# Storing the weight gradients of a decode block from GpSimd's queue instead of ScalarE's

## The chip, the cores and the metric

The kernel runs on one core of a Trainium2 chip. A core has five engines that each work through their own instructions in order: TensorE (PE in the profile, with its weight loads as PEld), VectorE (DVE), ScalarE (ACT), GpSimd (POOL) and SyncE (SP). They wait for each other by semaphores. Data move between the chip's memory (HBM) and the core's on-chip memory (SBUF) by DMA: an engine's sequencer issues a transfer into a DMA queue, sixteen DMA engines carry it out, and a semaphore tells when it has landed. SP's transfers go into queue q1 of the profile, ACT's into q10, and POOL's into q0.

The metric is the time of one execution on the device in microseconds (us), the median of several. Lower is better.

## The reference

One decode step of a small transformer block, forward and backward, in bfloat16. There are two sequences (B = 2) of one token each, a model width D of 640, 32 heads of 128, a cache of 4096 positions and an MLP of width 1728. Cut to what matters:

```python
def _A_ref(x, k_cache, v_cache, wq, wo):        # attention against a cache
    q = (x @ wq)  ->  heads
    p = softmax(q . k * 128**-0.5)
    return (p . v) @ wo
def _B_ref(x, w1, w2):                          # MLP
    return relu(x @ w1) @ w2

h   = x + _A_ref(layernorm(x), k_cache, v_cache, wq, wo)
out = h + _B_ref(layernorm(h), w1, w2)
# returned: out, and the gradients of (x, k_cache, v_cache, wq, wo, w1, w2) for a given grad_out
```

The caches have the shape 2 x 32 x 4096 x 128, so K, V and their two gradients are 64 tiles of 1 MB each, and these 256 MB are most of the traffic. The gradients of the four weights are outer products of rows that belong to the two tokens: `wq` (640 x 4096), `wo` (4096 x 640), `w1` (640 x 1728) and `w2` (1728 x 640). Together they are 15 MB, and it is their stores that the change touches.

## The kernel before

The work goes through the 64 pairs of sequence and head. In the first part (alone up to about 255 us, then beside the second) each pair's K and V are loaded (`Kt`, `Vt`), the scores are made by transposing K on TensorE (L440, copied out of PSUM by ACT in L445) and multiplying (L453), and the head's output is summed (L476). In the second part (`p2_iter`) V is loaded a second time for each pair (`Wt`), except for twelve pairs whose tile was kept. From it come the gradients of the probabilities (again L440, L445, L453 into `dp_ps`), from these the scores' gradient `gsp` on DVE (L874), and then the two 1 MB tiles `gK` and `gV`, which DVE writes (L860) and `store` (L881) sends out. From about 455 us on only the second part runs.

Beside this main line run three generators, of which a few steps are taken after each step of the main line (`bg_step`), by credits that are counted when the program is written. The order of the instructions on each engine is therefore fixed. One of the generators, `fin_gen`, makes the weight gradients once the values they need are there. It turns columns into rows (`rows_of`, L973, L978, L980), and `outer_rows` or `w2_rows` takes a tile `ot` of up to 1 MB, fills it piece by piece by `outer_tile` (TensorE multiplies into `o_ps`, L998, and ACT casts that into `ot`, L1004), and stores the tile when it is full (L1007). There are 19 such stores. Another generator, `gx_gen`, loads `wq` again in five tiles `wqs` (L1084) and multiplies them on DVE (`gxj`, L694), eight instructions to a tile.

What sets the order around the change:

- **Queues.** From about 490 us on (`alone`), `load_queue` is GpSimd's, so that `Wt`, `wqs` and `w_t` (L461, L1084, L380, L383) are issued by POOL, and the stores of `gK` and `gV` go through SP. Before that it is the other way round. The stores of `ot` are issued by ACT. POOL otherwise copies small vectors (`pp`, L905, and `pa`, L909) for the main line.
- **Buffers.** Tiles of 1 MB come from a stock that is shared out by purpose: `ld` for loads, `g` for `gK` and `gV`, `f` for `ot` (one at first, three later), `q` for `wqs`, `w_t` and two rows. An instruction that takes a tile waits until its last user, a store for instance, is done with it.
- **Completion semaphores.** In the built program every transfer signals one of eight semaphores, in turn, and a new transfer first waits until the last one with the same semaphore has landed. The transfers of SP and ACT share one set of eight; POOL's have a set of eight to themselves.

Of the kernel before, what the change touches and what calls it, by code (L numbers as in the profile page):

```python
# [15 lines left out]
def kernel(  # L16
# [20 lines left out]
    nc = tc.nc  # L37
# [35 lines left out]
    def pst(shape, dtype, role, name):  # L73

        k = banks[role].pop(0)
        banks[role].append(k)
        return ps.tile(shape, dtype, tag=f"bank{k}", bufs=1, name=name)
# [29 lines left out]
    def give(t, to=None, out=False):  # L107
        tag, k, _ = home_of.pop(id(t))
        if out:
            stored.add(k)  # L110
        to = to or goes_to(tag)
        owned[tag] -= 1
        owned[to] += 1
        free[to] += 1
        homes[to].append(k)
        given_at[k] = step[0]
# [872 lines left out]
    def outer_tile(todo, L, R, ot, stores):  # L989

        made = []
        for x in range(len(todo) + 1):
            if x < len(todo):
                sl, P, k, n0, nn = todo[x]
                q = 32 * (fw[0] % 4)
                o_ps = pst([128, 512], FP32, "o", "o_ps")
                fw[0] += 1
                nc.tensor.matmul(o_ps[0:P, 0:nn], lhsT=L[q:q + B, sl], rhs=R[q:q + B, n0:n0 + nn],  # L998
                                 start=True, stop=True)
                made.append((o_ps, P, k, n0, nn))  # L1000
                yield 0.3
            if x > 0:
                o_ps, P, k, n0, nn = made[x - 1]
                nc.scalar.copy(out=ot[0:P, k, n0:n0 + nn], in_=o_ps[0:P, 0:nn])  # L1004
                yield 0.3
        for out_ap, src in stores:
            nc.scalar.dma_start(out=out_ap, in_=src)  # L1007
        give(ot, out=True)

    def outer_rows(L, nrow, R, N, out_ap, cc):  # L1010


        P = nrow // cc
        grp = max(1, min(cc, 4096 // N))
        out_v = out_ap.rearrange("(p c) n -> p c n", c=cc)
        for c0 in range(0, cc, grp):
            gn = min(grp, cc - c0)
            while not rested("f", 13):
                yield 0.0
            ot = take("f", [128, grp, N], "ot")  # L1020
            todo = [(bass.ds(c0 + k, P, step=cc), P, k, n0, min(512, N - n0))
                    for k in range(gn) for n0 in range(0, N, 512)]
            yield from outer_tile(todo, L, R, ot, [(out_v[:, c0:c0 + gn, :], ot[0:P, 0:gn, :])])

    def w2_rows(L, R):

        out_v = out_7[0:NFF * 128, :].rearrange("(p c) n -> p c n", c=NFF)
        c0 = 0
        for gn in (5, 4, 4):
            while not rested("f", 13):  # L1030
                yield 0.0
            ot = take("f", [128, 6, D], "ot")
            last = c0 + gn == NFF
            cs = [(bass.ds(c0 + k, 128, step=NFF), 128, k) for k in range(gn)]
            if last and F_rem:
                cs.append((slice(NFF * 128, Dff), F_rem, gn))
            todo = [(sl, P, k, n0, min(512, D - n0)) for sl, P, k in cs for n0 in range(0, D, 512)]
            stores = [(out_v[:, c0:c0 + gn, :], ot[:, 0:gn, :])]
            if last and F_rem:
                stores.append((out_7[NFF * 128:Dff, :], ot[0:F_rem, gn, :]))  # L1040
            yield from outer_tile(todo, L, R, ot, stores)
            c0 += gn
# [314 lines left out]
```

## Time and profile before

| | |
|---|---|
| time of the kernel before | 888.31 us, median of 3 runs (886.6 to 888.36) |
| the profiled execution | 889.79 us, of which the span from the first to the last instruction is 888.0 us |
| busy: PE, DVE, ACT, POOL | 83%, 77%, 56%, 20% of the span |
| moved by DMA | 361.86 MB, 407 GB/s over the span |
| by queue: q1 (SP), q0 (POOL), q10 (ACT) | 264.49, 80.86 and 14.92 MB |
| granted TensorE clock | 0.773 on average, 0.5 to 0.7 from 490 us on |

An instruction in the profile has the line of the kernel, the engine, the operation and the tiles as out<-in. "Idle before <-releaser" is the time for which the engine had nothing to do, with what ended it. The DMA row gives the share of the sixteen DMA engines that were at work, in tenths for each of forty equal slices of 22.2 us, and as a fraction (1.00 is all sixteen) where a stretch of time is asked for; it can come out a little over 1, since packets of one engine can overlap. Beside the issue of a transfer the trace also has its sixteen signals of completion, one from each DMA engine.

### The profile page before, as it was taken

The numbers are of one execution on the slowest core, as the hardware profiler recorded it, in microseconds if no ns is written. First come the engines' busy times: TensorE is split into PE (matmuls) and PEld (weight loads), VectorE is DVE, ScalarE is ACT, GpSimd is POOL, SyncE is SP. The second block draws the span as 40 slices with busy tenths as digits, with TensorE's granted clock in tenths as the row PEclk, the third lists the DMA queues.
The fourth block names the chain that finished last, engine by engine and source line by source line (L and its number), as shares of the span: only waits on it lengthen the run. The fifth ranks groups of instructions, "written<-read, shape, count | busy, mean of one in ns | idle before, by whom it ended". The sixth has DMA issues, their size and how long they took to land.

```text
span 888.0 us, 24782 instructions
## 1 busy us (share of the span) xinstructions
PE 737.1 (83%) x10143; PEld 616.3 (69%) x10143; DVE 681.1 (77%) x1281; ACT 497.5 (56%) x1292; POOL 176.6 (20%) x309
## 2 busy tenths in 40 slices
PE   4999899899999998969858867878877898757593
PEld 4888788788887887858748756666666666544462
DVE  2666788877888886976778887878787779979763
ACT  1344343346777664645436868777656766545463
POOL 1344433443311000000022211110100211211000
PEclk9999999999999998999985556555556756556555
DMA  9999999999989999999999999999999999999986
GB/s 378 425 418 414 417 409 417 424 424 411 354 301 414 424 425 424 422 426 425 406 400 394 415 423 411 419 420 416 422 412 394 424 427 422 426 426 427 424 358 279
DMA packets 56146, 361.86 MB, mean 407 GB/s; under 512 B 5680, under 2 KB 11568, under 8 KB 15328
## 3 DMA queue, kind: packets, MB, share of 16 engines
q1 hardware_dynamic: 41640, 264.49, 72.0%
q0 software_dynamic: 11168, 80.86, 22.1%
q10 hardware_dynamic: 3224, 14.92, 4.1%
q8 instruction: 80, 1.31, 0.5%
q14 instruction: 34, 0.28, 0.1%
HBM read 211.11 MB, written 149.13 MB: 406 GB/s over the span
## 4 chain that ended last, share of the span: by engine, by line
DMA 37%; PE 35%; DVE 15%; ACT 7%; issue 4%; SPq 0%; ACTq 0%; POOL 0%; DVEq 0%; POOLq 0%
DMA Vt<-in_A_v_cache_dram 15%; PE t_ps L440 15%; DMA out_dram<-gK 11%; PE m_ps L476 8%; DMA out_dram<-gV 7%; DVE gK L860 4%; ACT gV L950 3%; DVE gV L860 3%; PE s_ps L453 3%; DMA wqs<-in_A_wq_dram 2%; DVE pk L486 2%; PE u_ps L514 2%; ACT t_sb L445 2%; PE dp_ps L453 2%; DVE gxj L694 1%
## 5 line engine op out<-in xcount | busy, mean ns | idle before, releaser
L445 ACT COPY t_sb<-t_ps 128x512 f32<-128x512 f32 x479 | 272.9, 587 | 194.3 <-PE t_ps L440 185.5
L453 PEld LDWEIGHTS <-t_sb 128*128 128x128 bf16 x4096 | 178.4, 102 | 66.5 <-ACT t_sb L445 39.6
L440 PE MATMUL t_ps<-ident_f,Wt 128*128 128x128 f32 x832 | 198.9, 390 | 1.1 <-ACT t_sb L445 1.1
L486 DVE TENSOR_TENSOR pk<-Kt,ep 128x2048 bf16<-128x2048 bf16 (+1 forms) x128 | 152.6, 1192 | 46.1 <-ACT ep L540 29.5
L476 PE MATMUL m_ps<-pk,Vt 128*128 128x129 bf16 x2048 | 171.0, 222 | 20.2 <-DMA Vt<-in_A_v_cache_dram 19.1
L860 DVE TENSOR_TENSOR gK<-rb,gsp 128x2048 bf16<-128x2048 bf16 x128 | 152.7, 1221 | 16.0 <-DMA out_dram<-gV 10.8
L476 PEld LDWEIGHTS <-Vt 128*128 128x128 bf16 x2048 | 124.7, 99 | 50.6 <-issue 28.6
L440 PEld LDWEIGHTS t_ps<-ident_f,Wt 128*128 128x128 f32 x832 | 138.6, 202 | 28.9 <-issue 22.0
L440 PE MATMUL t_ps<-ident_f,Kt 128*128 128x128 f32 x1024 | 155.0, 285 | 4.0 <-DMA Kt<-in_A_k_cache_dram 3.6
L860 DVE TENSOR_TENSOR gV<-rb,pp 128x2048 bf16<-128x2048 bf16 (+1 forms) x128 | 143.1, 1142 | 16.1 <-DMA out_dram<-gK 11.5
L453 PE MATMUL dp_ps<-gom,t_sb 128*128 128x2 bf16 x2048 | 95.9, 168 | 28.0 <-ACT t_sb L445 27.6
L440 PEld LDWEIGHTS t_ps<-ident_f,Kt 128*128 128x128 f32 x1024 | 113.2, 144 | 6.7 <-PE s_ps L453 3.9
L502 POOL COPY pk<-ep 128x16 bf16<-128x16 bf16 x80 | 84.5, 1058 | 155.7 <-ACT ep L540 80.9
L453 PE MATMUL s_ps<-qm,t_sb 128*128 128x2 bf16 x2048 | 87.4, 164 | 1.2 <-DVE t_sb L443 1.2
L1004 ACT CAST ot<-o_ps 128x512 bf16<-128x512 f32 (+3 forms) x152 | 67.7, 491 | 8.1 <-PE o_ps L998 5.3
L604 ACT CAST MT<-m_ps 128x128 bf16<-128x128 f32 x64 | 17.0, 265 | 93.4 <-PE m_ps L476 93.3
L461 POOL DMA_DIRECT2D Wt<-in_A_v_cache_dram x37 | 19.9, 539 | 223.3 <-PE t_ps L440 129.9
L903 ACT ACTIVATE rb<-dp_ps,rt 128x256 bf16<-128x256 f32 x64 | 30.2, 472 | 40.8 <-PE dp_ps L898 40.1
L694 DVE CUSTOM_DVE_ANT_0 hbc<-wo_t,hbc 128x640 bf16<-128x640 bf16 x64 | 52.7, 824 | 0.3
L874 DVE SCALAR_TENSOR_TENSOR gsp<-dp_ps,negdot,P_bf 128x64 bf16<-128x64 f32 x64 | 17.8, 278 | 45.0 <-PE dp_ps L453 45.0
L694 DVE CUSTOM_DVE_ANT_0 gxj<-wqs,gqr 128x1024 bf16<-128x1024 bf16 x40 | 48.8, 1220 | 1.6 <-DMA wqs<-in_A_wq_dram 1.5
L950 ACT ACTIVATE gV<-rb,pa 128x128 bf16<-128x128 bf16 x152 | 46.5, 392 | 4.6 <-DMA out_dram<-gK 4.1
(208 smaller groups left out, 752.8 us busy)
## 6 DMA issues: line engine op xcount, KB each, us to landing
Kt<-in_A_k_cache_dram SPq DMA_DIRECT2D x64, 1024.0 KB, 18.0
Vt<-in_A_v_cache_dram SPq DMA_DIRECT2D x64, 1024.0 KB, 17.3
out_dram<-gK SPq DMA_DIRECT2D x48, 1024.0 KB, 16.0
out_dram<-gV SPq DMA_DIRECT2D x47, 1024.0 KB, 17.0
Wt<-in_A_v_cache_dram POOLq DMA_DIRECT2D x37, 1024.0 KB, 11.2
out_dram<-gV POOLq DMA_DIRECT2D x17, 1024.0 KB, 9.8
out_dram<-gK POOLq DMA_DIRECT2D x16, 1024.0 KB, 10.4
Wt<-in_A_v_cache_dram SPq DMA_DIRECT2D x15, 1024.0 KB, 14.2
```

What stands on the lines that cost most here:

```text
L440: nc.tensor.transpose(t_ps[:, j, :], natf[:, 2 * cc:2 * cc + 2, :].rearrange("p c k -> p (c k)"), ident_f[:])
L445: nc.scalar.copy(out=t_sb[:], in_=t_ps[:])
L453: nc.tensor.matmul(dst[:, sc:sc + 2], lhsT=v[:, j, :, par], rhs=vecs[:, par, :], start=(par == 0), stop=(par == 1))
L461: load_queue().dma_start(out=t[:], in_=natural(A_k_cache if what == "K" else A_v_cache, *(turns if what == "W" else pairs)[i]))
L476: nc.tensor.matmul(r["m"][:, 0:129], lhsT=r["V"][:, sc, :], rhs=r["pk"][sc // HALF][:, sc % HALF, 0:129], start=(sc == 0), stop=(sc == NSC ...
L486: nc.vector.tensor_tensor(out=p["pk"][k][:, 0:n, 0:128].rearrange("p s (a two) -> p s a two", two=2), in0=p["K"][:, sl, :].rearrange("p s ...
L502: nc.gpsimd.tensor_copy(out=col, in_=e)
L694: nc.vector.tensor_tensor_reduce(out=junk[0:kc, 0:width], in0=in0, in1=in1, scale=1.0, scalar=0.0, op0=ALU.mult, op1=ALU.add, accum_out=acc)
L860: nc.vector.tensor_tensor(out=pairs_view(dst[:, sl, :]), in0=row.rearrange("p (a two) -> p a two", two=2)[:, None, :, :].to_broadcast([128 ...
L903: nc.scalar.activation(out=rb[:], in_=bank[:, 128:384], func=ACT.Copy, scale=rt[:, b, h:h + 1])
L950: nc.scalar.activation(out=gV[:, NSC - act + k, :], in_=c["rb"][:, 0:128], func=ACT.Copy, scale=pa[:, k:k + 1])
L1004: nc.scalar.copy(out=ot[0:P, k, n0:n0 + nn], in_=o_ps[0:P, 0:nn])
```

## The change

One line is changed. The store of a finished `ot` tile is issued by GpSimd's queue and not by ScalarE's.

```diff
@@ outer_tile @@
         for out_ap, src in stores:
-            nc.scalar.dma_start(out=out_ap, in_=src)
+            nc.gpsimd.dma_start(out=out_ap, in_=src)
         give(ot, out=True)
```

In the built program the 19 stores leave ACT's instructions and stand among POOL's, between the loads and copies that were issued around them; nothing else moves on any engine. A store now waits on POOL for ACT's last cast and for a semaphore of POOL's set; it shares queue q0 with the loads; and the eight semaphores that ACT and SP shared are SP's alone, but for the two small loads at the start.

## The prediction

> **What bounds the kernel now.** I read the page's DMA row first. All sixteen DMA engines are nearly always at work, so what matters is where they are not.
>
> ```profile
> DMA  9999999999989999999999999999999999999986
> GB/s 378 425 418 414 417 409 417 424 424 411 354 301 414 424 425 424 422 426 425 406 400 394 415 423 411 419 420 416 422 412 394 424 427 422 426 426 427 424 358 279
> ```
>
> The stores in question run from 567 us to the end, slices 26 to 40. There the ceiling of about 426 GB/s is held but for two slices near 660 us and the last two. So next come stretches of the end (columns: window, its length, then each engine's busy time, granted clock, DMA share, GB/s).
>
> ```profile
> 800.00:840.00 40.00, 25.99 (x204) 16.79 (x202) 35.09 (x54) 19.78 (x39) 4.00 (x7) 0.57 1.01 425
> 840.00:858.00 18.00, 14.96 (x132) 11.26 (x133) 10.04 (x11) 10.75 (x24) 0.47 (x2) 0.50 0.95 397
> 859.30:861.30 2.00, 2.00 (x16) 1.06 (x14) 0.79 (x2) 1.49 (x4) 0.00 (x0) 0.50 0.10 41
> 862.00:868.00 6.00, 5.57 (x43) 3.81 (x41) 3.42 (x4) 4.55 (x10) 0.00 (x0) 0.50 1.02 418
> 869.20:870.80 1.60, 1.60 (x9) 0.83 (x9) 1.60 (x2) 1.32 (x4) 0.00 (x0) 0.50 0.06 26
> 884.00:886.30 2.30, 0.00 (x0) 0.00 (x0) 0.00 (x0) 0.00 (x0) 0.00 (x0) 0.50 0.06 25
> ```
>
> The reader is to see the shares of 0.10 and 0.06. One engine of sixteen is 0.0625, and 425/16 is 26.6 GB/s: where fifteen DMA engines run dry, one goes on at full rate, to the very end. The sixteen completion signals of each store say the same. For the `gK` store issued at 863.18, fifteen came by 867.1 and the last at 873.1; for the one at 667.30, by 673.0 and at 682.1; for the one at 749.59, by 775.2 and at 786.2; for the last one, at 878.50, by 884.3 and at 886.8. After 873.1 six stores were left to this engine: `gV`, `ot`, `gK`, `gV`, `ot` and `gK`, five of 1024 KB and one `ot` of 512. A sixteenth of them is 352 KB, 360,000 bytes, in the 13.7 us to 886.8: 26.3 GB/s. It never waits for work. I call it the late engine; the last signal already trailed the median by about 5 us at 545 us, before the first `ot` store (545.63: median 553.3, last 558.7).
>
> The waits of ACT come third, as they are what the change removes.
>
> ```profile
> 774.30 0.58 ACT L445 COPY t_sb<-t_ps 128x512 f32<-128x512 f32 x1 [3.64 <-DMA out_dram<-gK]
> 791.60 0.22 ACT L973 COPY wide<-x1c 128x32 bf16<-128x32 bf16 x1 [9.23 <-DMA out_dram<-gV]
> 840.94 0.22 ACT L973 COPY wide<-GQc 128x32 bf16<-128x32 bf16 x1 [5.10 <-DMA out_dram<-gV]
> ```
>
> Each stands right behind an `ot` store (773.91, 791.22, 840.55). ACT had finished casting and waited for a semaphore of the shared eight, held by one of SP's slow stores: 37 us in q1 for `gK` of 749.59. The third wait holds up the end: PE and DVE wait too (DVE's `gsp` at 842.75 after 5.54 us idle), and from 841 to 875 the chain of waits runs through PE and ACT alone.
>
> Last, how the queues share (queue, packets, MB, share of the sixteen engines), first from 712 to 744 us, then from 744 to 756.
>
> ```profile
> q1 hardware_dynamic: 774, 5.60, 41.5%
> q0 software_dynamic: 770, 5.34, 39.6%
> q10 hardware_dynamic: 431, 2.62, 19.7%
> ...
> q1 hardware_dynamic: 350, 2.56, 50.5%
> q0 software_dynamic: 349, 2.49, 49.8%
> ```
>
> Two queues with work get half each; a third takes from both.
>
> **The change part by part.**
>
> *ACT.* It loses 19 issues of 0.34 us (row of L1007), 6.5 us, and about 0.4 us before the next instruction each time, since the store waits for its own cast (0.41 and 0.42 us idle after the stores at 733.27 and 874.35). It loses the semaphore waits: 3.64 + 9.23 + 0.53 (818.28) + 5.10 = 18.5 us. The first three lie where DVE is busy 45 of 50 us (750 to 800) and waits for nothing of ACT's but 1.7 us; they hide behind DVE. The last, 5.1 us, and two issues of 0.4 us lie on the chain that ends the compute: 5.9 us. The wait of 1.72 us for an `ot` buffer (648.98) stays, or shrinks.
>
> *POOL.* It gains 19 issues at the 0.54 us of its own rows, 10.3 us on an engine that is busy 20%. Behind each stand a `Wt` load, a `pp` copy or `wqs`. `Wt` lands 16.5 to 60 us before its first transpose from 574 us on, `pp` is done 3.3 us or more before its `gV` where it stands behind a store: hidden. The wait for ACT costs nothing where POOL waits later anyway (105 us in all for `t_ps`). The wait for its own set means the eighth transfer before; that has landed in each case but at the load of 743.51, a few us.
>
> *Queue q0.* From 709.84 to 737.77, 2.56 MB (MB here of 1024 KB) of `ot` go ahead of the third `wqs`. Of 32 us from 712, q0 moved 5.34 MB; at half of 425 GB/s it moves 6.8 but has 5.34 + 2.62 = 7.96 to move, so it is 1.16 MB, 5.5 us, behind. The third `wqs` landed at 755.8 and was first used at 759.05: 3.2 us of slack, so DVE would stall by 2.3 us. Adding up queues with equal shares and the issue times of before, I get 6.2 us late for this one, 8.6 for the fourth (slack 7.4 us) and 3.2 for the last (slack 16). Take 3 us for the third and 1.2 for the fourth: 4.2 us, bounds 0 and 12 (if all 2.56 MB counted at 213 GB/s).
>
> *Queue q1.* It gets half where it had a third: by the same sum `gK` and `gV` land 6 to 11 us earlier between 723 and 787 us. DVE's waits for these buffers there (0.84, 1.93, 0.19, 1.74) are 4.7 us and go. So up to 837 us DVE comes out about even: 4.2 lost, 4.7 won, and the first `wqs` (DVE waited 1.47 us for it) lands 1 us earlier.
>
> *The end.* By compute the last `gK` would be issued 5.9 us earlier than 878.50. But the late engine's work is the same bytes from the same stores, and it reached that last `gK` at 884.2 with earlier stores' data before it all the time. Transfers arrive earlier, and it finishes when it finishes: at 886.4. The other fifteen, idle 6 us between 849 and 871, close up and end earlier than 882.1, and nobody waits for them. Sum: 0 from the late engine, and the compute's 5.9 us turn into a longer queue in front of it. If compute came out later instead, the first 2 us would cost nothing: from issue to first packet it was 0.9 to 3.9 us for the fifteen `ot` stores that found q10 empty, 3.6 for most, and 878.5 + 3.6 is 882.1, 2.1 us ahead of 884.2.
>
> That the late engine stays as it is can't be read off before: what makes it late is not shown. Its share of every store is a sixteenth on either queue (sixteen signals each), and packets take the same on both (8192 bytes in 309 ns on q0 and q1). I therefore take 0; bounds are -5.9 (it was not what held the end) and +3.9 (below).
>
> The profiled execution took 889.79 us for a span of 888.0, 1.5 above the median of 888.31. I apply the sum to the median: 888.3 us. About 0.2%, 1.8 us, is what a measurement of this kernel can tell from no change.
>
> **One rule of the skill, against the change.** The Trainium skill, page "SBUF — State Buffer", section "SBUF: two separate sides", says that a DMA from GpSimd's queue has its descriptors written by GpSimd's cores, which a VectorE operation in a two-port mode locks out; it gives about 620 ns alone and 3100 ns beside such an operation. By these figures each store would start about 2.5 us later, an estimate from that page, and the time would be as in the third rival. The trace bears no sign of it: POOL's issues take 0.53 to 0.57 us beside a DVE busy at 90%, and 33 stores of `gK` and `gV` that POOL issued before 490 us landed in about 10 us (9.8 and 10.4 in the page's list, 17.0 and 16.0 for SP's).
>
> **The rivals.**
>
> 1. *Faster, because compute holds the end.* If the late engine is an accident of this execution, or its surplus goes with queue q10, the end follows the last store: 888.3 - 5.9 = 882.4 us, and 880 with part of DVE's 4.7 us. For it: the chain of waits, which runs through PE and ACT for 34 us. Against it: a share of 0.06 to the end. 0.28.
> 2. *Slower, because `wqs` queues behind the stores.* Place: DVE's `gxj` at the third and fourth `wqs`, between 757 and 785 us, where DVE is the busiest engine. Price: at the upper bound of 12 us late, less 3.2 of slack, 8.8 us, and 3 more at the fourth, 11.8. ACT's 5.9 and the 2.1 us before the late engine come off: +3.8, 892.1 us. It decides once DVE loses over 8 us net; the middle value is under zero. 0.17.
> 3. *Slower, because GpSimd's descriptors wait for DVE.* Say each of the three stores ahead of the third `wqs` is held for two DVE instructions of 1.22 us: 7.3 us more on the 3 us above, 10.3, less 5.9 and 2.1: +2.3, 890.6 us. 0.03.
>
> That the stores would not move is excluded by the built program.
>
> **How the numbers follow.** No change to be told, 0.52, at 888.3; its own range is 886.5 to 890.1. Rival 1 gives faster, 0.28; rivals 2 and 3 slower, 0.20. The range of 882 to 891.5 takes in most of rival 1 and the lower half of rival 2, and leaves out some 0.17.
>
> **What would show it.** ACT's waits for `out_dram<-gK` and `<-gV` are gone. q10 has nothing after the start and q0 14.9 MB more. POOL has 19 issues at L1007 of 0.54 us. The third `wqs` takes 20 us or more and DVE waits for it by 0 to 4 us; DVE's waits for `gK` and `gV` after 770 us shrink. DVE's last `gK` comes 3 to 8 us earlier, and the stretch at the end with a DMA share of 0.06 grows from 2 to 4 us towards 8. I am wrong if the span ends with the last store and not with one engine's rest, or if DVE's wait for `wqs` is 8 us or more.

## The result, and the profile after

The changed kernel took 894.45 us (median of four runs, 893.3 to 896.72) where the kernel before took 887.59 on the same chip: a ratio of 1.0066, 95% interval 1.0044 to 1.0088. Twelve more runs of it gave 896.39 us and 1.0073 (1.0047 to 1.0099). It is slower by about 0.7%. The two medians lie 6.9 us apart, which would be 1.0077; the ratio on record is 1.0066, about 6 us, and the record doesn't show how it is formed. Forecast was 888.3, no change. The profiled execution took 893.7 us for a span of 891.9.

What the change does directly came out as forecast. These are the queues on the page of the changed kernel (queue, packets, MB, share of the sixteen engines), and, from the answer on the tile `ot`, the nineteen issues (ns: min/median/max, first and last start):

```profile
q1 hardware_dynamic: 41640, 264.49, 72.0%
q0 software_dynamic: 14240, 95.77, 26.1%
...
q10 hardware_dynamic: 40, 0.01, 0.0%
```

```profile
L1007 POOL DMA_DIRECT2D out_dram<-ot x19: 539/539/726, 569.3 to 869.8; - x19
```

ScalarE's queue is empty, each issue takes POOL 0.54 us. ScalarE's waits for `gK` and `gV` stores are gone. In the timeline of ACT, the `wide` copies, one of which waited 5.10 us at 840.94 before, now come without such a wait:

```profile
839.85 0.23 ACT L973 COPY wide<-GQc 128x32 bf16<-128x32 bf16 x1
840.11 0.59 ACT L445 COPY t_sb<-t_ps 128x512 f32<-128x512 f32 x1
840.78 0.59 ACT L980 CAST GQr<-rw_ps 128x512 bf16<-128x512 f32 x1
842.82 0.59 ACT L445 COPY t_sb<-t_ps 128x512 f32<-128x512 f32 x1 [1.46 <-PE t_ps L440]
843.30 0.22 ACT L973 COPY wide<-GQc 128x32 bf16<-128x32 bf16 x1
```

And the compute does end earlier: the last `gK` store is issued at 873.29 us instead of 878.50. Yet the span ends 3.9 us later. Two places show where it went. The first is DVE's wait for the third `wqs`, in the list of waits from 700 to 880 us and in DVE's timeline:

```profile
DVE gxj L694 <- DMA wqs<-in_A_wq_dram: 7.5, 1, 7.5
```

```profile
757.03 1.22 DVE L860 TENSOR_TENSOR gK<-rb,gsp 128x2048 bf16<-128x2048 bf16 x1
765.78 1.23 DVE L694 CUSTOM_DVE_ANT_0 gxj<-wqs,gqr 128x1024 bf16<-128x1024 bf16 x1 [7.53 <-DMA wqs<-in_A_wq_dram]
```

In this execution DVE made the loss good: its `gsp` at 772.0 us is 6.7 us later than the same one before, the one at 807.7 only 0.1. The second place is the DMA row, slices 36 and 37 and the last:

```profile
DMA  9999999999979999999999999999999999999994
GB/s 379 424 419 415 416 406 418 426 423 397 339 296 404 424 423 426 423 425 425 413 406 392 419 420 419 405 419 421 422 424 406 418 423 422 423 415 401 423 420 207
```

All DMA engines are at work in slices 36 and 37, but move 415 and 401 GB/s instead of 426 and 427. A window shows it better (columns: window, length, busy time of each engine, granted clock, DMA share, GB/s), first before, then after:

```profile
780.00:820.00 40.00, 23.16 (x232) 16.89 (x230) 34.27 (x47) 19.40 (x44) 4.88 (x8) 0.63 1.01 426
```

```profile
780.00:820.00 40.00, 29.59 (x252) 21.44 (x252) 39.76 (x56) 22.14 (x50) 8.41 (x11) 0.59 1.01 405
820.00:840.00 20.00, 15.65 (x126) 11.43 (x127) 19.14 (x32) 12.20 (x27) 2.80 (x6) 0.50 1.01 424
840.00:877.00 37.00, 27.70 (x220) 18.27 (x218) 20.59 (x22) 21.25 (x42) 3.77 (x5) 0.50 1.01 422
877.50:885.00 7.50, 0.00 (x0) 0.00 (x0) 0.00 (x0) 0.00 (x0) 0.00 (x0) 0.50 0.36 153
886.70:890.90 4.20, 0.00 (x0) 0.00 (x0) 0.00 (x0) 0.00 (x0) 0.00 (x0) 0.50 0.06 23
```

21 GB/s less over 40 us is 0.84 MB, and at 26.6 GB/s for one DMA engine that is 32 us of one engine's work. It is not shared by all sixteen. At the end most engines run dry at 877.4 us, but others need until 885 (share 0.36, some six engines), and one until 890.9 (0.06). Before, one alone was late by more than 2 us.

The sixteen completion signals of the last `gK` store, in us, tell the same:

```
          issued   first   median  the last four
before    878.50   882.3   882.4   882.5 882.5 884.3 886.8
after     873.29   877.4   879.5   885.4 885.4 886.6 891.0
```

The median engine is 2.9 us earlier than before, the last one 4.2 us later. The packets' durations show when these engines lost their time. Between 780 and 825 us 116 data packets took at least 1.4 times their usual length (8192 bytes of a `gK` or `gV` store mostly 0.60 us instead of 0.31, 5120 bytes of an `ot` store 0.37 instead of 0.20); before there were two. Of those in GpSimd's queue all but two have the sizes of `ot` stores; the loads in the same queue kept their length. Together the 116 took 28 us longer than usual, which is nearly the 32 us worked out above. Between 805 and 818 us the long packets come to 2.8 engines' time.

### The profile page after: what moved, and what is told of

Its sections match the earlier page's. It is cut to its first block, busy times and chain, and to the rows that moved or that the text cites. A ratio compares the mean times of both kernels' runs of the same rounds, so it can differ in the third digit from the quotient of the medians.

```text
span 891.9 us, 24846 instructions
## 1 busy us (share of the span) xinstructions
PE 739.3 (83%) x10143; PEld 617.9 (69%) x10143; DVE 681.0 (76%) x1281; ACT 498.4 (56%) x1292; POOL 188.6 (21%) x328
## 4 chain that ended last, share of the span: by engine, by line
PE 37%; DMA 25%; DVE 22%; ACT 7%; issue 5%; SPq 0%; ACTq 0%; DVEq 0%; POOL 0%; POOLq 0%
PE t_ps L440 15%; DMA Vt<-in_A_v_cache_dram 11%; PE m_ps L476 9%; DVE gK L860 6%; DMA wqs<-in_A_wq_dram 6%; DVE gV L860 5%; DMA out_dram<-gV 4%; DMA out_dram<-gK 4%; DVE gxj L694 4%; ACT gV L950 3%; PE s_ps L453 3%; PE u_ps L514 3%; DVE pk L486 3%; ACT t_sb L445 2%; PE dp_ps L453 2%
## 5 line engine op out<-in xcount | busy, mean ns | idle before, releaser
L440 PE MATMUL t_ps<-ident_f,Wt 128*128 128x128 f32 x832 | 201.8, 394 | 1.5 <-ACT t_sb L445 1.5
L860 DVE TENSOR_TENSOR gV<-rb,pp 128x2048 bf16<-128x2048 bf16 (+1 forms) x128 | 142.9, 1141 | 13.6 <-DMA out_dram<-gK 9.1
## 6 DMA issues: line engine op xcount, KB each, us to landing
Kt<-in_A_k_cache_dram SPq DMA_DIRECT2D x64, 1024.0 KB, 18.7
```

The source lines that it names most:

```text
L440: nc.tensor.transpose(t_ps[:, j, :], natf[:, 2 * cc:2 * cc + 2, :].rearrange("p c k -> p (c k)"), ident_f[:])
L860: nc.vector.tensor_tensor(out=pairs_view(dst[:, sl, :]), in0=row.rearrange("p (a two) -> p a two", two=2)[:, None, :, :].to_broadcast([128 ...
```

## The experiments

One number goes through all runs, and I call it the spread: from the first to the last of the sixteen signals of one load, as a mean over the `Wt` and `wqs` loads issued between 760 and 820 us. It tells how far the DMA engines have drifted apart in the queue of the loads (this is what drift means below): 2.5 us before, 10.8 us after. "Long packets" are those of at least 1.4 times their usual length between 700 and 840 us: 12 before, 157 after. First the two kernels themselves and the change cut in two.

**The changed kernel again** (no edit).

> The changed kernel itself, profiled a second time. Three theories for why its span ended 3.9 us later (891.9 against 888.0) although its last store was issued 5.2 us earlier. Theory A: the stores in GpSimd's queue make the DMA engines drift apart; in the first profile 8192-byte packets of the gK and gV stores took 0.6 us instead of 0.31 on some four engines between 797 and 818 us, and from 877.4 us on fewer than 14 engines were busy. If that belongs to the change, the second profile shows packets of doubled length again, more than 50 of them between 780 and 825 us or in another stretch with ot stores, a last store issued near 873 us, a drain of 10 us or more and a span of 890 to 894. Theory B: which engines run late is an accident of an execution. Then the second profile has fewer than 15 such packets and a span of 886 to 889 us, and only the median time stays 4 to 7 us above the kernel before. Theory C: the wait of 7.5 us of DVE for the third wqs is the cost. Then the drain follows the last gK store's issue by no more than 9 us in the second profile, and the last gK is issued after 878 us.

Measured: long packets again, 220 of them, 139 between 780 and 825 us; spread 17.7 us. The end, in windows:

```profile
882.20:888.40 6.20, 0.00 (x0) 0.00 (x0) 0.00 (x0) 0.00 (x0) 0.00 (x0) 0.50 0.38 159
888.60:890.30 1.70, 0.00 (x0) 0.00 (x0) 0.00 (x0) 0.00 (x0) 0.00 (x0) 0.50 0.10 43
890.60:895.80 5.20, 0.00 (x0) 0.00 (x0) 0.00 (x0) 0.00 (x0) 0.00 (x0) 0.50 0.06 25
```

The drain, from the first signal of the last `gK` (882.3) to its last (895.9), is 13.6 us long, and the span is 896.8: theory A, and B is out. But the last `gK` was issued at 878.17, not near 873, since DVE waited 12.4 us for the third `wqs` and made good only part of it; the wait that theory C names is real too. The span was above the forecast of 894 for that reason.

**The kernel before again** (no edit, one run, 890.38 us).

> The kernel before, profiled a second time. Theory A (drift comes with the stores in GpSimd's queue): fewer than 15 packets of doubled length between 700 and 890 us, the last gK store issued at 878 to 879 us, one DMA engine late by 4 to 9 us, span 886.5 to 889.5. Theory B (accident): the late engine is missing, or several engines are late, and the span differs from 888.0 by more than 2 us.

Measured: 42 long packets, seven of them between 780 and 825 us; last `gK` issued at 876.34, fifteen signals by 882.7 and the last at 887.3; spread 3.8 us; span 888.5. The one late engine is there again, late by 4.6 us, and it is alone. The count of long packets was above the 15 forecast, so that the count by itself is a rough sign.

**The last six stores alone on GpSimd's queue.** `last_rows` is set where the work on `out_4` begins.

```diff
-            nc.gpsimd.dma_start(out=out_ap, in_=src)
+            (nc.gpsimd if last_rows[0] else nc.scalar).dma_start(out=out_ap, in_=src)
```

> Only the last six of the 19 stores (those of out_4, from about 810 us on) are issued from GpSimd's queue, the first thirteen from ScalarE's as before. By then only few Wt loads are left in GpSimd's queue. Theory A: the packets of doubled length between 780 and 825 us are gone (fewer than 15), the last gK store is issued 5 to 6 us earlier than 878.5, and the time is that of the kernel before or better: 883 to 888.5 us. Theory C: also no cost, as wqs lands as before (third one at 755 to 757 us, DVE waits less than 1 us for it). Theory B: no forecast for the drain, the time is within 2 us of the kernel before. If the six stores themselves cost the 6.9 us, the time is 893 to 896.

Measured: 888.5 us, 1.0003 (0.9983 to 1.0023). Spread 4.3 us, six long packets between 780 and 825 us. Compute ended 7.3 us earlier than before (last `gK` issued at 871.21), and the last signal came at 887.1, as late as before. The windows of the end:

```profile
877.80:882.00 4.20, 0.00 (x0) 0.00 (x0) 0.00 (x0) 0.00 (x0) 0.00 (x0) 0.50 0.19 82
882.30:884.60 2.30, 0.00 (x0) 0.00 (x0) 0.00 (x0) 0.00 (x0) 0.00 (x0) 0.50 0.13 57
885.20:887.00 1.80, 0.00 (x0) 0.00 (x0) 0.00 (x0) 0.00 (x0) 0.00 (x0) 0.50 0.04 18
```

Two engines work to 884.7 (0.13) and one to the end. So the last six stores are not the loss, and compute that ends 7 us earlier is worth nothing: the prediction's main step, seen alone. A gain of up to 5 us was inside the expectation and did not come. (DVE's one wait for `wqs`, 4.2 us, was for the first of them, at 721.6; the third landed at 757.4 and nothing waited for it.)

**The first thirteen alone on GpSimd's queue.**

```diff
-            nc.gpsimd.dma_start(out=out_ap, in_=src)
+            (nc.scalar if last_rows[0] else nc.gpsimd).dma_start(out=out_ap, in_=src)
```

> The converse: the first thirteen stores are issued from GpSimd's queue and the last six from ScalarE's. Theory A: the packets of doubled length come back (over 50 between 780 and 825 us), and the time is 892 to 896 us, as for the changed kernel. Theory C: DVE's wait for the third wqs is 6 to 9 us and the last gK is issued later than in the changed kernel, as ACT's wait of some 5 us at the last wide copy may return: 893 to 899 us. If the loss lies with the last six, the time is 886 to 889.

Measured: 894.33 us, 1.0065 (1.0038 to 1.0092): the whole loss. 197 long packets, spread 18.7 us. The profiled execution took 903.02 us, 8.7 above the median; in it DVE waited for `wqs` twice:

```profile
DVE gxj L694 <- DMA wqs<-in_A_wq_dram: 14.1, 2, 13.4
```

So the last `gK` was issued at 889.72, 11.2 us later than before, and its last signal came 10.5 us after that, against 8.3 before: in this profile most of the loss is DVE's wait, as theory C had it, beside the long packets of theory A.

**The six stores of `out_5` alone on GpSimd's queue**, those between about 705 and 790 us.

```diff
-            nc.gpsimd.dma_start(out=out_ap, in_=src)
+            (nc.gpsimd if stage[0] == 1 else nc.scalar).dma_start(out=out_ap, in_=src)
```

> Only the six stores of out_5 (from about 710 to 790 us), 5.0 MB, are issued from GpSimd's queue, the seven before and the six after them from ScalarE's. If the loss is made where the wqs and Wt loads meet these six stores (theories W and S alike), the third wqs makes DVE wait 6 us or more, over 50 packets of doubled length lie between 700 and 840 us, and the time is 891 to 896 us. If the seven stores before 680 us are needed for the engines to fall behind, fewer than 25 such packets are seen, DVE waits 2 to 4 us for the third wqs (the fair-share sum), and the time is 886 to 889.5.

Measured: 892.63 us, 1.0040 (1.0016 to 1.0065). 90 long packets, spread 11.1 us, a wait of 6.5 us for the third `wqs`:

```profile
DVE gxj L694 <- DMA wqs<-in_A_wq_dram: 8.6, 2, 6.5
```

By the medians these six stores, which meet the `wqs` and `Wt` loads, make more than half of the loss, though the interval leaves room for 0.16% to 0.65%. The profiled execution took 888.31 us, 4.3 below the median, and in it the last signal came at 885.4: a spread of 11.1 us in the loads' queue does not by itself make the end late.

**The `wqs` loads taken out of that queue.** All stores as in the change, but the five `wqs` loads on ScalarE's queue.

```diff
-                load_queue().dma_start(out=t[:], in_=wq_r[:, len(tiles), :])
+                nc.scalar.dma_start(out=t[:], in_=wq_r[:, len(tiles), :])
```

> All 19 stores in GpSimd's queue as in the change, but the five wqs loads are issued from ScalarE's queue, which the change had emptied, so that no wqs stands behind a store. Two theories remain for the 6 us. Theory W (the wqs queue): the loss is DVE's wait for the third wqs, 7.5 and 12.4 us in the two profiles of the changed kernel. Then the third wqs lands within 14 us of its issue, DVE waits less than 2 us for it, and the time is that of the kernel before or less, 882 to 888.5 us. Theory S (spread of the DMA engines): the stores in GpSimd's queue make some of the sixteen DMA engines fall behind, with packets of doubled length, and the end waits for the last engine whatever DVE does. Then over 50 packets of doubled length are seen again between 700 and 840 us, the sixteen signals of the Wt loads after 780 us lie 5 us or more apart, and the time stays at 890 to 895 although DVE waits for no wqs.

Measured: 892.01 us, 1.0031 (1.0012 to 1.0050). The third `wqs` landed 11.5 us after its issue and DVE waited for none: theory W's condition is met, and its time is not. 122 long packets, a spread of 6.0 us, last signal at 891.7 for a last `gK` issued at 876.53. Theory S, then, but not alone: about half of the loss, 1.0073 less 1.0031, went with the `wqs`, and here the spread is smaller too, so that its share and that of DVE's wait are not told apart by this run. (The two intervals, 1.0012 to 1.0050 and 1.0047 to 1.0099, just touch, so the half is rough.)

**All loads taken out of that queue.** Stores on GpSimd's queue as in the change, loads (`Wt`, `w2`, `wqs`) on ScalarE's.

```diff
-        return nc.gpsimd if alone[0] else nc.sync
+        return nc.scalar if alone[0] else nc.sync
```

> All 19 stores in GpSimd's queue, and all loads of the second half (Wt, w2, wqs) issued from ScalarE's queue, so that loads and stores are in different queues again but the stores are in GpSimd's. Theory S1 (it is loads and stores in turn in one queue that make engines fall behind): fewer than 25 packets of doubled length between 700 and 840 us, and signals of the Wt loads within 3 us of one another. Theory S2 (it is stores from GpSimd's queue as such): more than 50 such packets, and the sixteen signals of the ot stores lie 5 us or more apart. The time decides nothing between them, since ScalarE now has 0.34 us for each load and the waits for the loads' buffers: 886 to 900 us.

Measured: 888.8 us, 1.0005 (0.9988 to 1.0023). The loss is gone with the stores still on GpSimd's queue. Spread 2.6 us, the signals of the `ot` stores of the same stretch within 2.7. The long packets, 41, lie between the two forecasts, 32 of them in SP's queue and four in GpSimd's. S1 by the spread; the time, which was to decide nothing, goes with it. The last `gK` was issued at 873.49, the last signal came at 885.0. In the profile of the changed kernel these were 873.29 and 891.0: compute ended at the same time, and the 6.0 us are the end of the transfers alone. From 780 to 820 us DVE and PE were as busy as there, and the rate was 422 GB/s where it was 405, so that busier engines are not what slowed the packets:

```profile
780.00:820.00 40.00, 29.83 (x261) 22.70 (x260) 39.76 (x56) 21.89 (x50) 5.32 (x6) 0.54 1.01 422
```

**All nineteen stores on SP's queue**, behind `gK` and `gV`; GpSimd's queue has loads alone.

```diff
-            nc.gpsimd.dma_start(out=out_ap, in_=src)
+            nc.sync.dma_start(out=out_ap, in_=src)
```

> All 19 stores issued from SP's queue, behind the gK and gV stores, so that one queue has all stores and GpSimd's has loads alone. ScalarE is free of stores as in the change. Both S1 and S2: fewer than 25 packets of doubled length between 700 and 840 us, the signals of the Wt loads within 3 us of one another, the third wqs landing before 756 us, the last gK issued at 870 to 875 us, and a time of 883 to 889 us, set by the one late DMA engine. Against it: if the longer queue of SP holds the buffers of gK and gV, DVE waits for these by 5 us or more between 720 and 800 us, and the time is 889 to 893.

Measured: 890.52 us, 1.0022 (1.0003 to 1.0040), 22 long packets, spread 2.1 us, third `wqs` at 750.8. Compute ended earliest of all, with the last `gK` issued at 870.28, 8.2 us ahead of the kernel before, and the last signal came at 886.8 as there:

```profile
877.60:881.00 3.40, 0.00 (x0) 0.00 (x0) 0.00 (x0) 0.00 (x0) 0.00 (x0) 0.50 0.43 183
882.00:886.70 4.70, 0.00 (x0) 0.00 (x0) 0.00 (x0) 0.00 (x0) 0.00 (x0) 0.50 0.06 24
```

One engine works for the last 4.7 us. The median is 1.5 us above the forecast's upper end, and what makes the 0.2% isn't shown.

**The mirror on ScalarE's queue.** The kernel before, with the loads of the second half on the queue of its `ot` stores.

```diff
-        return nc.gpsimd if alone[0] else nc.sync
+        return nc.scalar if alone[0] else nc.sync
```

> The mirror of the change on another queue: the 19 stores stay in ScalarE's queue, and the loads of the second half (Wt, w2, wqs) are issued from ScalarE's queue too, so that one queue holds loads and stores in turn beside SP's queue of stores, as in the changed kernel, but it is not GpSimd's. If a mixed queue beside a queue of stores makes the DMA engines fall behind, whichever queue it is: over 80 packets of doubled length between 700 and 840 us with the larger part after 780 us, the sixteen signals of the Wt loads after 780 us 5 us or more apart, the third wqs late by 6 us or more against the kernel before, and a time of 891 to 897 us. If it takes GpSimd's queue: fewer than 50 such packets, signals of Wt within 3 us, the third wqs late by the backlog alone, and a time of 886 to 891 us.

Measured: 894.23 us, 1.0064 (1.0041 to 1.0087). 94 long packets, 62 of them between 780 and 825 us; spread 12.1 us. Some 30 of the 62 are loads that start together at 804 to 808 us, so that the spread is the better sign here as well. GpSimd's queue moves nothing in this half, and the engines drift apart all the same, at a rate of 409 GB/s:

```profile
780.00:820.00 40.00, 28.17 (x257) 21.27 (x256) 36.11 (x49) 21.61 (x51) 4.40 (x4) 0.59 1.01 409
```

Against the run with the loads alone on ScalarE's queue, only the stores' queue differs: 888.8 us where loads and stores are apart, 894.23 where they share. Here ScalarE also issues the loads and waits for their buffers and semaphores, and DVE waits for `wqs` by only 0.5 us; the third `wqs` is issued 9.4 us late and lands at 766.4, eight us after its median signal:

```profile
DVE gxj L694 <- DMA wqs<-in_A_wq_dram: 0.5, 1, 0.5
```

So the drift and the lower rate come with a queue of loads and stores beside SP's queue of stores, and don't need GpSimd's. How much of the 0.64% they make isn't shown: from 700 us on ScalarE waited 31.5 us for transfers to land, against 18.4 before, the last `gK` was issued 1.7 us later than before (6.7 later than with the loads alone on ScalarE's queue), and of the sixteen engines only two ended the last store late (886.1 and 889.2), as before (884.3 and 886.8).

**Loads in SP's queue**, between `gK` and `gV`, with `ot` on ScalarE's queue as before.

```diff
-        return nc.gpsimd if alone[0] else nc.sync
+        return nc.sync
```

> The kernel before (stores of ot in ScalarE's queue) with the loads of the second half (Wt, w2, wqs) issued from SP's queue, between the gK and gV stores, so that loads and stores are in turn in one queue again, but not in GpSimd's. If any queue that holds loads and stores in turn makes DMA engines fall behind, over 50 packets of doubled length lie between 700 and 840 us, and the sixteen signals of the Wt loads lie more than 5 us apart on average. If that belongs to GpSimd's queue, fewer than 50 such packets are seen; the spread of the signals then is that of the gK and gV stores (one engine late). The loads wait behind 25 us of stores in either case, and the wqs with them, so the time is above that of the kernel before by 5 us or more: 893 to 920 us.

Measured: 896.78 us, 1.0075 (1.0050 to 1.0100), as forecast for loads that wait behind stores. 110 long packets, by which a mixed queue would be to blame in general, but spread 3.1 us, by which it would not. The two signs part here: most of these packets came when the engines had all stood idle (715 to 722 us) and started with loads together. At the end all sixteen engines finished the last store within 0.2 us of one another. So loads and stores in turn in one queue are not enough; loads were seen to drift by more than 5 us on average only where their queue also took stores and ran beside another one full of stores.

All profiled executions side by side (the time is the median of all runs, the other columns are of the one profile; the ratio is against the kernel before on the same chip):

| kernel | loads / `ot` in queue of | spread, us | GB/s, 780 to 820 us | last `gK` issued | last signal | time, us | ratio |
|---|---|---|---|---|---|---|---|
| before | GpSimd / ScalarE | 2.5 | 426 | 878.50 | 886.8 | 887.59 | 1 |
| before, again | GpSimd / ScalarE | 3.8 | 425 | 876.34 | 887.3 | 890.38 (one run) | |
| last six moved | GpSimd / 13 ScalarE, 6 GpSimd | 4.3 | 425 | 871.21 | 887.1 | 888.50 | 1.0003 |
| loads apart | ScalarE / GpSimd | 2.6 | 422 | 873.49 | 885.0 | 888.80 | 1.0005 |
| `ot` on SP | GpSimd / SP | 2.1 | 424 | 870.28 | 886.8 | 890.52 | 1.0022 |
| `wqs` apart | GpSimd (`wqs` ScalarE) / GpSimd | 6.0 | 413 | 876.53 | 891.7 | 892.01 | 1.0031 |
| `out_5` moved | GpSimd / 13 ScalarE, 6 GpSimd | 11.1 | 416 | 875.97 | 885.4 | 892.63 | 1.0040 |
| mirror | ScalarE / ScalarE | 12.1 | 409 | 880.18 | 889.2 | 894.23 | 1.0064 |
| first 13 moved | GpSimd / 13 GpSimd, 6 ScalarE | 18.7 | 407 | 889.72 | 900.2 | 894.33 | 1.0065 |
| after | GpSimd / GpSimd | 10.8 | 405 | 873.29 | 891.0 | 894.45 | 1.0066 |
| after, again | GpSimd / GpSimd | 17.7 | 401 | 878.17 | 895.9 | 896.39 | 1.0073 |
| loads on SP | SP / ScalarE | 3.1 | 426 | 886.01 | 895.2 | 896.78 | 1.0075 |

In the first five rows the last `gK` is issued at anything from 870.3 to 878.5, and the last signal comes between 885.0 and 887.3. No kernel here is faster than the one before. The rate parts the cases without exception: 422 GB/s or more in the first five rows and the last, 416 or less in the six where stores joined the loads in a queue beside SP's. (The last six stores start at 818 us and hardly fall into this stretch.)

One thing the change did not bring. The `gK` and `gV` stores issued from 760 to 820 us in SP's queue have their own signals 13.8 us apart on average in the kernel before and 13.6 in the changed one, and 7 us or more apart in every run but the one with the loads on SP's queue (3.2). Engines that are apart in SP's queue of stores were there from the start; new with the change are loads that share in such a lag, several late engines in place of one, and the lower rate.

## Why the prediction was wrong

- **ACT: right.** The 19 issues and the waits for `gK` and `gV` stores are gone, and compute ended 5.2 us earlier (forecast 5.9) in the first profile.
- **POOL: right.** 19 issues of 0.54 us. PE waited for no `Wt`.
- **Queue q1: right.** `gK` of about 749 us took 26.0 us to land instead of 36.6, 11 us earlier.
- **Queue q0: right in place, too small.** The third `wqs` was to land 6.2 us late with a stall of 2.3 to 3 us. Counted from its issue, the median signal came after 25.9 us (26.3 in the second profile) instead of 16.5, so that the backlog alone was 9.4 us; the last of the sixteen came another 2.8 and 7.4 us after the median, 1.5 before. DVE waited 7.5 and 12.4 us, the second above the upper bound of 12. That engines could drift apart within this queue was in no term.
- **The end: the step that failed.** "The late engine's work is the same bytes from the same stores ... it finishes when it finishes: at 886.4." One half held: where loads and stores kept queues of their own, the last signal stayed at 885.0 to 887.3 with compute 2 to 8 us earlier. The other half, that the engine stays as late as it is, did not. I had put 0 on it, with 3.9 as the upper bound; in its place the runs showed +4.2 and +9.1 us at the last signal, and several more engines late beside it: four signals of the last `gK` or more came 5 us behind the median or later in either profile, where at most one had before. That the loss at the end comes with the stores in the loads' queue is shown by the run with the loads apart, where compute ended at the same time (873.49 us), the last signal came at 885.0 and the median time was 888.80. Part of the +9.1 is compute, which ended 4.9 us later there than in the first profile.
- **The sign I had named** was a last stretch with a share of 0.06 that grows to 8 us. It was 4.2 us of 0.06, behind 7.5 us of 0.36. Of the signs of being wrong, DVE's wait of 8 us or more for `wqs` was just missed in the first profile (7.5) and met in the second (12.4).
- **Rival 1 (compute holds the end): out**, by the stores moved last and by SP's queue: 7.3 and 8.2 us of compute were worth nothing.
- **Rival 2 (`wqs` behind the stores): its mechanism is there, at its place**, but not as its account had it, with the decision at 8 us of DVE's net loss: in the first profile DVE's net loss was 0.1 us by 808 us, and the time was 6 us up. Without the `wqs` in that queue, 0.31% of 0.73% was left.
- **Rival 3 (descriptors wait for DVE): out.** An issue took 0.54 us, and the first signal of the store of 864.65 came 4.2 us later, against 3.7 from ScalarE's queue (870.00 before). The Trainium skill's figure of 3100 ns, on the page named in the prediction, was not met in these issues; whether a VectorE operation in a two-port mode ran beside them the rows don't tell.

Of two further statements on the page "DMA: Bandwidth & Descriptors" of the Trainium skill one is at odds with these runs. Its section "Issuing engines are not separate DMA queues" says that issuing from several engines only saves the time of the issuing itself. Here the queue that the stores share decided about 0.6%: 888.8 us with the loads in another queue, against 894.45 in the changed kernel, with the same transfers and compute that ended at the same time. Its section "Latency and other measured facts" holds two of the sixteen engines usually slower, and guesses at the descriptor rings of GpSimd's queue. The records here carry no engine's number; in the mirror run, without any transfer of GpSimd's in that half, one engine ended 3.1 us after the other fifteen all the same, so those transfers aren't needed for a late engine.

What stays open is why the engines drift. In the changed kernel the long packets of that stretch are stores' packets, in both queues and on a few engines at a time; what makes them long isn't shown, and in the two runs with the loads on SP's queue or beside the stores on ScalarE's many of them are loads after a pause, so that their count does not follow the drift. Nor is it known why one engine is late in the kernel before.

## What to carry to other kernels

Where the DMA engines are busy throughout and the last of them sets the end, an engine freed of waits need not buy anything (7.3 and 8.2 us of earlier compute bought nothing here), and what a moved transfer does to the spread of the engines must be priced: read the first, median and last of the sixteen signals in the queue that it joins, not the bytes alone. Before merging two kinds of transfers into one queue, try the same move with the other kind taken out of it; here, on top of the change, that one line made the difference between 1.0066 and 1.0005. Profile the changed kernel twice: its two profiles had the same cause and ends 4.9 us apart.

## What had not been expected of the hardware

- In the changed kernel some DMA engines ran stores at half speed for about 20 us (most of the long packets lie between 797 and 818 us) while the others went on at full rate: 8192 bytes in 0.60 us instead of 0.31, with all sixteen still showing as busy (share 1.01) and the rate at 405 instead of 426 GB/s.
- In the first profile the lag did not go away again. From 818 us on nearly all packets had their usual length again (11 long ones up to 877 us), the share was 1.01 throughout, and three engines were 6 to 8 us behind the median in the `gK` store issued at 820.0 us, beside the latest, and 6 to 7 us behind it in the last. That they are the same three the records, without engine numbers, don't show.
- With loads and stores in one queue beside SP's queue of stores, the signals of the loads spread over 10.8 to 18.7 us (6.0 where `wqs` was taken out); with the loads in a queue of their own, 2.1 to 3.8; with loads and stores in SP's own queue, 3.1.
